# Two scatters behind a branch, two turns of gathered rows moved up, and GpSimd's memsets ahead of the first gathers

## The chip, the cores and the metric

The kernel runs on one core of one Trainium2 chip. The metric is device microseconds of a whole execution, median of several runs. TensorE (PE in the profile) multiplies matrices, VectorE (DVE) and ScalarE (ACT) work on tiles of 128 partitions, GpSimd (POOL) does element-wise work too and issues the DMAs whose rows are picked by an index, and SyncE (SP) issues plain DMAs. Each engine runs its own queue in order; semaphores hold the queues together.

## The reference

The input `x` has 8 sequences of 2496 rows with 256 channels. The first part multiplies each channel's spectrum with a complex filter:

```python
X = np.fft.rfft(x, axis=1)
Y = X * (filt_r + 1j * filt_i)[None, :, :]
y = np.fft.irfft(Y, n=x.shape[1], axis=1)
```

The second part takes the 19968 rows of `y` as tokens of a mixture of 8 experts, with a capacity of 80 tokens each:

```python
logits = x @ w_gate
expert_idx = np.argmax(logits, axis=1)
gate_w = softmax(logits)[arange, expert_idx]
out = zeros((N, D))
for e in range(E):
    tok_idx = the tokens of expert e, at most `capacity` of them with the largest gate_w
    h = np.maximum(x[tok_idx] @ w1[e], 0.0)
    out[tok_idx] = gate_w[tok_idx, None] * (h @ w2[e])
```

So at most 640 of the 19968 output rows are not zero.

## The kernel before

The Fourier transform is done by matmuls with tables. A sequence is read in six chunks (`load_x`, line 299, issued by SyncE). `stage1` (line 310) multiplies eleven pairs of columns, steps k = 0 to 10, with a small table; the results go to the tile `t1` by copies on ScalarE, for the first sequence on VectorE at every third step (line 324). `transpose1` (line 326) turns them, and `stage2` (line 338) multiplies with the second table and then, on VectorE and GpSimd, with the filter. `turn` (line 366) turns the products and gets the gating logits from them. This runs step by step over all 8 sequences, and the order of the work on each engine is the order in which the source writes it, under a manual schedule (from line 809).

The filter comes in five blocks of rows in `fst`. `load_filter(v, half)` (line 273) issues two gathers on GpSimd, of real rows (half 0) or imaginary rows (half 1); `sign_filter(v)` (line 281) multiplies the imaginary rows with a sign on ScalarE, in two passes; `turn_filter` (line 287) transposes them on TensorE. At the start GpSimd issues the four gathers of block 0 (lines 851 and 852), clears its tiles (`lg`, `zero_t`, two `z`, `key`, `kt`; line 854), copies the identity twice, and waits with a one-element copy to `mark` (line 858) for the fourth chunk of `x` before it gathers blocks 1 and 2. `sign_filter(0)` stands in ScalarE's queue behind step 6 of the first sequence.

`zero_t` is the source of the 64 DMAs that fill the output with zeros, one at a time through the first part. The tokens are picked while the last sequences run, and the picked rows are computed back from the spectra into the DRAM tile `y_sel`.

The experts come last (class `Experts`, line 1129). For each expert, `gather` (line 1144) fetches its rows, `turn` (line 1158) transposes them on TensorE into `px`, which VectorE copies to `xs`; `layer1` (line 1176) is 16 products to PSUM, which ScalarE and VectorE bring to `hT`; `layer2` (line 1192) is 8 products, a scaling by the gate on ScalarE into `ys`, and a scatter of 80 rows to `out` on GpSimd (line 1208). For the first three experts the gathered rows lack those of the last sequence; `turn` adds them by two more matmuls with `yr` and `last`. The order is written out in lines 1033 to 1048. For expert 7 `layer2` gets `keep=ys_last`: the result stays in a slice of `zero_t`, and its scatter stands at the end of the kernel (line 1126).

Between them is a branch (lines 1087 and 1088): if the fast way of picking failed (`bad` is not 0), a general path computes all again. With this input it isn't taken, but every engine reads `bad` and passes the branch; on the path that skips the body each engine also raises its semaphores by what the body would have added, GpSimd those of its DMA queues too (INC_SWDGE_SEM in the profile), after it has waited for its own DMAs ahead of the branch. In the built program each scatter waits for the landing of the scatter ahead of it, as they all write `out`.

Of the kernel before, what the change touches and what calls it, by code (L numbers as in the profile page):

```python
# [15 lines left out]
I32 = mybir.dt.int32  # L16
# [7 lines left out]
B, S, C = 8, 2496, 256  # L24
# [12 lines left out]
E, FF = 8, 1024  # L37
# [44 lines left out]
def kernel(  # L82
# [11 lines left out]
    nc = tc.nc  # L94
# [9 lines left out]
                                  name=f"rows{h}_tbl") for h in range(2)]  # L104
# [5 lines left out]
    consts = ctx.enter_context(tc.tile_pool(name="consts", bufs=1))  # L110
# [22 lines left out]
    lg = consts.tile([128, NP, NA, E], F32, name="lg")  # L133
# [57 lines left out]
    zero_t = zp.tile([128, ZR * C // 128], F32, name="zero_t")  # L191
# [9 lines left out]

    idxs = consts.tile([cap, E], I32, name="idxs")
    idxg = consts.tile([cap, E], I32, name="idxg")
    idx_last = consts.tile([cap, 1], I32, name="idx_last")
    ys_last = zero_t[0:cap, 0:C]
    gate = consts.tile([cap, E], F32, name="gate")
    idxt = consts.tile([cap, E], I32, name="idxt")
    idxb = consts.tile([128, B], I32, name="idxb")
# [26 lines left out]
    zs = [consts.tile([128, 2, E, SP], F32, name=f"z_{i}") for i in range(2)]  # L235
    key = consts.tile([128, 48, E], F32, name="key")
    kt = consts.tile([128, 2, N2, 4], F32, name="kt")

    with ExitStack() as actx:
# [33 lines left out]
        def load_filter(v, half):  # L273
            k, filt = half, (filt_r, filt_i)[half]
            for i in range(2):
                nc.gpsimd.indirect_dma_start(
                    out=fst[:, v, 2 * k + i, :], out_offset=None, in_=filt[:, :],
                    in_offset=bass.IndirectOffsetOnAxis(
                        ap=frow[:, 2 * v + i:2 * v + i + 1], axis=0))
# [254 lines left out]
        def pt(shape, dt, name, rnd):  # L534
            return sp.tile(shape, dt, name=f"{name}_{rnd}", tag=name)
# [214 lines left out]
        def pick_slots(part):  # L750
            f_t = st["f_t"]
            if part == 0:
                off_e = pt([128, 1], F32, "off_e", 1)
                nc.vector.tensor_copy(out=off_e[:], in_=st["poff"][:, 2, 0:1])
                slot = pt([128, KR], F32, "slot", 1)
                nc.vector.tensor_scalar(out=slot[:], in0=iota[:, 0:KR], scalar1=off_e[:, 0:1],
                                        scalar2=None, op0=AL.add)
                st["slot"] = slot
            elif part == 3:
                slot = st["slot"]  # L760
                st["eplc"] = xpool.tile([128, KR, cap], BF16, name="eplc", tag="x")
                nc.vector.tensor_tensor(
                    out=st["eplc"][:], in0=slot[:].unsqueeze(2).to_broadcast([128, KR, cap]),
                    in1=iota[:, 0:cap].unsqueeze(1).to_broadcast([128, KR, cap]),
                    op=AL.is_equal)
            elif part == 1:
                st["eval"] = pt([128, KR, 4, E], BF16, "eval_", 1)
                for i in range(4):
                    nc.gpsimd.tensor_tensor(
                        out=st["eval"][:, :, i, :],  # L770
                        in0=f_t[:, i, :].unsqueeze(2).to_broadcast([128, KR, E]),
                        in1=ehot[:].unsqueeze(1).to_broadcast([128, KR, E]), op=AL.mult)
            elif part == 2:
                pe = st["misc"][0:cap, 128:128 + 4 * E]
                for k in range(KR):
                    nc.tensor.matmul(pe, lhsT=st["eplc"][:, k, :],
                                     rhs=st["eval"][:, k].rearrange("p v e -> p (v e)"),
                                     start=(k == 0), stop=(k == KR - 1))
                es = st["es"] = pt([cap, 4, E], F32, "es", 1)
                nc.vector.tensor_copy(out=es[:].rearrange("p v e -> p (v e)"), in_=pe)  # L780
                nc.vector.scalar_tensor_tensor(out=idxg[:], in0=es[:, 1, :], scalar=128.0,
                                               in1=es[:, 0, :], op0=AL.mult, op1=AL.add)
                emp = pt([cap, E], F32, "emp", 1)
                nc.vector.tensor_scalar(out=emp[:], in0=es[:, 3, :], scalar1=st["off"][0:cap, 0:1],
                                        scalar2=float(N + S), op0=AL.is_le, op1=AL.mult)
                tokens(nc, sp, cap, es[:, 1, :], 0.0, es[:, 2, :], es[:, 3, :], -1.0, emp, idxs,
                       idxt)
                nc.vector.tensor_copy(out=idx_last[:], in_=idxs[:, E - 1:E])
            else:
                es = st["es"]  # L790
                inl = pt([cap, NO], F32, "inl", 1)
                nc.vector.tensor_scalar(out=inl[:], in0=es[:, 1, 0:NO], scalar1=float(B - 1),
                                        scalar2=None, op0=AL.is_equal)
                nc.vector.scalar_tensor_tensor(out=inl[:], in0=es[:, 0, 0:NO], scalar=1.0,
                                               in1=inl[:], op0=AL.add, op1=AL.mult)
                diag = fp.tile([cap, NO, cap], BF16, name="diag", bufs=1)
                nc.vector.tensor_tensor(
                    out=diag[:], in0=ident[0:cap, 0:cap].unsqueeze(1).to_broadcast([cap, NO, cap]),
                    in1=inl[:].unsqueeze(2).to_broadcast([cap, NO, cap]), op=AL.mult)
                last = st["last"] = fp.tile([128, NO, cap], F32, name="last", bufs=1)  # L800
                pd = st["misc"][:, 192:192 + NO * cap]
                nc.tensor.matmul(pd, lhsT=ones_bf[0:cap, :], start=True, stop=True,
                                 rhs=diag[:].rearrange("p e t -> p (e t)"))
                nc.vector.tensor_scalar(
                    out=last[:].rearrange("p e t -> p (e t)"), in0=pd, scalar1=pid[:, 0:1],
                    scalar2=1.0, op0=AL.subtract, op1=AL.is_equal)

        LATE, LEAD = 2, 2
        with tc.manual_schedule():
# [3 lines left out]
            for cb in range(NDB):  # L813
                nc.scalar.dma_start(out=gi[:, cb, 128:128 + E],
                                    in_=moe_w_gate[128 * cb:128 * cb + 128, :])
# [16 lines left out]
            def put_s1():  # L832
                if s1:
                    b, k = s1.pop(0)
                    stage1(b, k)
                    if (2 * k + 2) % JC == 0 or k == NB - 1:
                        free[0] += 1
# [10 lines left out]
            for _ in range(NX0 - NCH):  # L848
                load_x(*xs.pop(0))
            free[0] = 0  # L850
            load_filter(0, 0)
            load_filter(0, 1)
            for t in (lg, zero_t, *zs, key, kt):
                nc.gpsimd.memset(t[:], 0.0)
            nc.gpsimd.tensor_copy(out=gi[:, 0, 0:128], in_=ident[:])
            nc.gpsimd.tensor_copy(out=gi[:, 1, 0:128], in_=ident[:])
            mark = tpool.tile([1, 1], F32, name="mark")
# [4 lines left out]
            load_filter(2, 1)  # L862
            for k in range(NB):
                put_s1()
                if k == 6:
                    sign_filter(0)
                if k == 7:
                    load_d(1)
                    put_x(-1)
# [130 lines left out]
            for part in range(5):  # L1000
# [20 lines left out]
            ex = Experts(nc, cap, ident, fp, lambda n: fps.tile([128, 512], F32, name=n, tag="f"),  # L1021
                         lambda n: yps.tile([128, 2, 512], F32, name=n, tag="y"),
                         y_sel[0:128 * B, :], out, idxg, idxs, gate, w1s, w2s, homes=homes)
# [7 lines left out]
            ex.extra = st["yr"], st["last"]  # L1031

            ex.turn(0)
            ex.layer1(0)
            ex.turn(1)
            for e in range(E):
                if e + 3 < E:
                    ex.gather(e + 3)
                if e == 0:
                    ex.layer2(0)  # L1040
                if e + 1 < E:
                    ex.layer1(e + 1)
                if e + 2 < E:
                    ex.turn(e + 2)
                if e > 0:
                    ex.layer2(e, keep=ys_last if e == E - 1 else None)
                if e + 6 < E:
                    weights(e + 6, wpool, "w")

# [38 lines left out]
    with tc.If(n_bad > 0):  # L1088
# [22 lines left out]
        with (  # L1111
# [5 lines left out]
            ex = Experts(nc, cap, ident, fp3, lambda n: px3.tile([128, 512], F32, name=n, tag="f"),  # L1117
                         lambda n: ph3.tile([128, 2, 512], F32, name=n, tag="y"), y_sel, out,
                         idxg, idxs, gate, w1s, w2s, "g")
            for e in range(E):  # L1120
# [2 lines left out]
                ex.turn(e)  # L1123
                ex.layer1(e)
                ex.layer2(e)
    scatter(nc, out, ys_last, idx_last[:])


class Experts:
# [78 lines left out]
def scatter(nc, out, ys, idx):  # L1208
    nc.gpsimd.indirect_dma_start(  # L1209
        out=out[:, :], out_offset=bass.IndirectOffsetOnAxis(ap=idx, axis=0), in_=ys,  # L1210
        in_offset=None, bounds_check=N - 1, oob_is_err=False)
# [400 lines left out]
```

## Time and profile before

| | us |
|---|---|
| median of 3 runs (461.26 to 462.69) | 461.64 |
| profiled execution | 453.17 |
| its span, first to last instruction | 451.4 |
| TensorE busy, of the span | 431.9 |
| first 20 us: TensorE busy | 16.15 |
| experts, 381 to 440: TensorE busy | 58.5 |
| behind the last matmul, 440 to 451.4 | 11.4 |

The span is what the lines and timelines show; the profiled execution has 1.8 us around it. The runs without a profile have a longer median than the profiled one. A line of a timeline has the start in us, the duration, the engine, the line of the source, the operation, the tiles, and in brackets how long the engine sat idle before it and what ended that. A busy time says little by itself here, as TensorE is busy nearly all the time: what counts is what TensorE waits for, and what follows its last matmul.

The order of the experts' work on TensorE, one item each (t turn, 1 and 2 the layers, with the expert's number), is this before:

```
t0 1.0 t1 2.0 1.1 t2 1.2 t3 2.1 1.3 t4 2.2 ... 1.7 2.6 2.7
```

### The profile page before, as it was taken

What the parts mean: (1) busy time and instruction counts of PE and PEld (TensorE: products, weight loads), DVE (VectorE), ACT (ScalarE), POOL (GpSimd) and SP (SyncE); (2) the same over time, 40 slices, a digit from 0 to 9 for tenths busy, and PEclk for the clock granted to TensorE, in tenths of its full rate; (3) what the DMA queues carried; (4) which work ended last, traced back from release to release, by engine and by line L of the source; (5) the groups of instructions that cost most, each with busy time, mean ns of one, the idle gap of its engine ahead of it and who ended that gap; (6) DMA issues with size and microseconds to landing.
All of it is one profiled execution on the core that took longest, in us unless ns stands there. A gap on an engine that the chain in (4) does not pass through costs nothing. (4 is left out here: it accounts for less than half of the span.)

```text
span 451.4 us, 8713 instructions
## 1 busy us (share of the span) xinstructions
PE 431.9 (96%) x3389; PEld 406.6 (90%) x3389; DVE 194.2 (43%) x577; ACT 219.5 (49%) x359; POOL 178.5 (40%) x244
## 2 busy tenths in 40 slices
PE   7899999999999999999999999999999999999990
PEld 5899999999999999999999998888888888888870
DVE  2565544445654545754546789478300000110100
ACT  3576766666766666766666644332223321111110
POOL 8687343342543443443444456220754002112110
PEclk9999999999999999999999999999999999999997
DMA  7867345999988987878991222996989972999100
GB/s 206 278 178 226 65 129 180 325 293 359 351 244 253 328 265 231 290 241 254 362 395 79 95 94 99 366 359 257 355 320 362 396 255 77 374 367 369 36 20 12
DMA packets 39701, 109.96 MB, mean 244 GB/s; under 512 B 5297, under 2 KB 14832, under 8 KB 38882
## 3 DMA queue, kind: packets, MB, share of 16 engines
q1 hardware_dynamic: 28688, 76.41, 50.6%
q10 hardware_dynamic: 6466, 21.05, 11.9%
q0 software_dynamic: 4496, 11.85, 8.0%
q8 instruction: 29, 0.48, 0.4%
q14 instruction: 22, 0.18, 0.1%
HBM read 68.97 MB, written 43.20 MB: 249 GB/s over the span
## 5 line engine op out<-in xcount | busy, mean ns | idle before, releaser
L358 POOL TENSOR_TENSOR p<-p,p 128x256 f32<-128x256 f32 x154 | 110.0, 736 | 134.3 <-DVE p L351 93.1
L351 DVE TENSOR_TENSOR p<-pb,ft 128x512 f32<-128x512 f32 x160 | 102.2, 680 | 11.0 <-PE pb L343 10.9
L324 ACT COPY t<-pa 128x480 f32<-128x480 f32 x84 | 83.8, 1002 | 26.1 <-PE pa L317 25.7
L317 PE MATMUL pa<-wf_t,x 117*128 117x120 f32 x704 | 91.2, 276 | 3.4 <-DMA x<-in_x_dram 3.0
L317 PEld LDWEIGHTS pa<-wf_t,x 117*128 117x128 f32 x704 | 84.9, 192 | 5.1 <-DMA x<-in_x_dram 1.8
L371 PE MATMUL py<-gi,p 128*128 128x136 f32 x640 | 87.8, 280 | 1.3 <-POOL p L358 0.7
L343 PE MATMUL pb<-d_t,t 128*128 128x128 f32 x640 | 85.2, 276 | 0.2
L371 PEld LDWEIGHTS py<-gi,p 128*128 128x128 f32 x640 | 79.8, 190 | 1.7 <-POOL p L358 1.0
L343 PEld LDWEIGHTS pb<-d_t,t 128*128 128x128 f32 x640 | 78.0, 192 | 1.1 <-PE py L371 0.4
L334 ACT COPY t<-pt 128x512 f32<-128x512 f32 x80 | 46.7, 585 | 59.8 <-PE pt L332 58.4
L520 PE MATMUL po<-yb,wt 128*128 128x256 f32 x240 | 56.6, 380 | 0.3 <-ACT wt L513 0.3
L394 DVE COPY z<-py 128x16 f32<-128x16 f32 x60 | 11.2, 187 | 86.6 <-ACT ysp L387 57.9
L332 PE MATMUL pt<-ident,t 128*128 128x128 f32 x320 | 47.9, 273 | 0.4 <-DVE t L324 0.4
L520 PEld LDWEIGHTS po<-yb,wt 128*128 128x128 f32 x240 | 43.4, 190 | 5.3 <-ACT wt L513 0.5
L513 ACT COPY wt<-pw 128x512 f32<-128x512 f32 x39 | 22.7, 585 | 47.4 <-PE pw L508 45.3
L332 PEld LDWEIGHTS pt<-ident,t 128*128 128x128 f32 x320 | 37.5, 141 | 0.6 <-issue 0.6
L387 ACT COPY ysp<-py 128x512 f32<-128x512 f32 x60 | 35.4, 591 | 0.0
L1182 PEld LDWEIGHTS ph<-xs,w 128*128 128x128 f32 x256 | 29.7, 192 | 1.7 <-DVE xs L1173 1.1
L1182 PE MATMUL ph<-xs,w 128*128 128x80 f32 x256 | 29.8, 275 | 0.8 <-DVE xs L1173 0.8
L1197 PE MATMUL po<-w,hT 128*80 128x256 f32 x128 | 28.8, 379 | 0.0
L1197 PEld LDWEIGHTS po<-w,hT 128*80 128x80 f32 x128 | 18.6, 150 | 7.5
L1188 DVE TENSOR_SCALAR hT<-ph 128x320 f32<-128x320 f32 x8 | 3.9, 491 | 47.9 <-ACT hT L1187 47.9
(204 smaller groups left out, 339.5 us busy)
## 6 DMA issues: line engine op xcount, KB each, us to landing
out_dram<-zero_t SPq DMA_DIRECT2D x64, 312.0 KB
x<-in_x_dram SPq DMA_DIRECT2D x40, 468.0 KB
w<-in_moe_w_dram SPq DMA_DIRECT2D x16, 1024.0 KB
yf<-ysp ACTq DMA_DIRECT2D x30, 512.0 KB
yb<-yf SPq DMA_DIRECT2D x6, 2560.0 KB
yf<-ys ACTq DMA_DIRECT2D x10, 512.0 KB
x<-in_x_dram SPq DMA_DIRECT2D x8, 234.0 KB
d_t<-d_tbl SPq DMA_DIRECT2D x5, 256.0 KB
```

Source lines behind the costliest of these rows:

```text
L317: nc.tensor.matmul(out=ps[:, i, :, 2 * NS * cb:2 * NS * cb + 2 * NS], lhsT=xt[0:NJ * N1, (2 * k + i) % JC, 128 * cb:128 * cb + 128], rhs=w ...
L324: copy(out=t1[:, 2 * k - h:2 * k - h + 2], in_=ps[:])
L332: nc.tensor.transpose(ps[:, i, cb, :], t1[:, a:a + 2, :].rearrange("p r n -> p (r n)"), ident[:])
L334: nc.scalar.copy(out=t2[:].rearrange("p i c -> p (i c)"), in_=ps[:].rearrange("p i c q -> p (i c q)"))
L343: nc.tensor.matmul(out=ps[:, cb, i], rhs=d_t[:, 2 * u + i, :], start=True, stop=True, lhsT=t2[:, i, 128 * cb:128 * cb + 128])
L351: nc.vector.tensor_tensor(out=pt, in0=ps[:].rearrange("p c s r q -> p (c s) r q"), in1=f.unsqueeze(2).to_broadcast([128, 2 * NDB, 2, NQ]), ...
L358: adder.tensor_tensor(out=yt[:, :, r, :], in0=yt[:, :, r, :], in1=pr[1][:, :, 1 - r, :], op=op)
L371: nc.tensor.matmul(out=ps[:, i, ZW * cb:ZW * cb + ZW], rhs=gi[:, cb, :], lhsT=yt[:, 2 * cb + i].rearrange("p r q -> p (r q)"), start=True, ...
L387: nc.scalar.copy(out=dst.rearrange("p s (h w) -> p s h w", h=2), in_=pv[:, :, :, 0:128])
L520: nc.tensor.matmul(pos[t][:, 0, 0:C], lhsT=wts[t, g // 2][:, g % 2, i, :], rhs=ybs[t][:, s, :], start=(s == 0), stop=(s == NS - 1))
L1182: nc.tensor.matmul(ph[:, fc // 4, fc % 4, 0:cap], lhsT=self.w1s[e][:, k, 128 * fc:128 * fc + 128], rhs=xs[:, k, :], start=(k == 0), stop=( ...
L1197: nc.tensor.matmul(po[0:cap, :], lhsT=hT[:, fc, :], rhs=self.w2s[e][:, fc, :], start=(fc == 0), stop=(fc == NFC - 1))
```

## The change

Four edits:

- The results of experts 6 and 7 are both kept, in two slices of `zero_t`, and both are scattered behind the branch, with their two columns of indices in `idx_last`. Before it was expert 7's alone.
- `turn(1)` is moved ahead of expert 0's layer 1 and `turn(2)` directly behind it. TensorE's order becomes `t0 t1 1.0 t2 2.0 1.1 1.2 t3 2.1 1.3 ...`; from turn 3 on it is the same.
- GpSimd clears its six tiles ahead of the four gathers of filter block 0 instead of behind them.
- `sign_filter(0)` stands behind step 8 instead of step 6 in ScalarE's queue.

Nothing else moves in any engine's queue.

```diff
@@ -201,8 +201,9 @@
 
     idxs = consts.tile([cap, E], I32, name="idxs")
     idxg = consts.tile([cap, E], I32, name="idxg")
-    idx_last = consts.tile([cap, 1], I32, name="idx_last")
-    ys_last = zero_t[0:cap, 0:C]
+    NL = 2
+    idx_last = consts.tile([cap, NL], I32, name="idx_last")
+    ys_last = [zero_t[0:cap, C * i:C * i + C] for i in range(NL)]
     gate = consts.tile([cap, E], F32, name="gate")
     idxt = consts.tile([cap, E], I32, name="idxt")
     idxb = consts.tile([128, B], I32, name="idxb")
@@ -785,7 +786,7 @@
                                         scalar2=float(N + S), op0=AL.is_le, op1=AL.mult)
                 tokens(nc, sp, cap, es[:, 1, :], 0.0, es[:, 2, :], es[:, 3, :], -1.0, emp, idxs,
                        idxt)
-                nc.vector.tensor_copy(out=idx_last[:], in_=idxs[:, E - 1:E])
+                nc.vector.tensor_copy(out=idx_last[:], in_=idxs[:, E - NL:E])
             else:
                 es = st["es"]
                 inl = pt([cap, NO], F32, "inl", 1)
@@ -848,10 +849,10 @@
             for _ in range(NX0 - NCH):
                 load_x(*xs.pop(0))
             free[0] = 0
+            for t in (lg, zero_t, *zs, key, kt):
+                nc.gpsimd.memset(t[:], 0.0)
             load_filter(0, 0)
             load_filter(0, 1)
-            for t in (lg, zero_t, *zs, key, kt):
-                nc.gpsimd.memset(t[:], 0.0)
             nc.gpsimd.tensor_copy(out=gi[:, 0, 0:128], in_=ident[:])
             nc.gpsimd.tensor_copy(out=gi[:, 1, 0:128], in_=ident[:])
             mark = tpool.tile([1, 1], F32, name="mark")
@@ -862,7 +863,7 @@
             load_filter(2, 1)
             for k in range(NB):
                 put_s1()
-                if k == 6:
+                if k == 8:
                     sign_filter(0)
                 if k == 7:
                     load_d(1)
@@ -1031,8 +1032,9 @@
             ex.extra = st["yr"], st["last"]
 
             ex.turn(0)
+            ex.turn(1)
             ex.layer1(0)
-            ex.turn(1)
+            ex.turn(2)
             for e in range(E):
                 if e + 3 < E:
                     ex.gather(e + 3)
@@ -1040,10 +1042,10 @@
                     ex.layer2(0)
                 if e + 1 < E:
                     ex.layer1(e + 1)
-                if e + 2 < E:
+                if 2 < e + 2 < E:
                     ex.turn(e + 2)
                 if e > 0:
-                    ex.layer2(e, keep=ys_last if e == E - 1 else None)
+                    ex.layer2(e, keep=ys_last[e - E + NL] if e >= E - NL else None)
                 if e + 6 < E:
                     weights(e + 6, wpool, "w")
 
@@ -1123,7 +1125,8 @@
                 ex.turn(e)
                 ex.layer1(e)
                 ex.layer2(e)
-    scatter(nc, out, ys_last, idx_last[:])
+    for i in range(NL):
+        scatter(nc, out, ys_last[i], idx_last[:, i:i + 1])
 
 
 class Experts:
```

## The prediction

> **What bounds the kernel now.** I read the page's busy times first, then a table of stages, then the waits of TensorE, and then, stage by stage, the timelines of the places that the change touches.
>
> ```profile
> PE 431.9 (96%) x3389; PEld 406.6 (90%) x3389; DVE 194.2 (43%) x577; ACT 219.5 (49%) x359; POOL 178.5 (40%) x244
> ```
>
> TensorE is busy for 96% of the span of 451.4 us. So work taken off another engine is worth nothing unless TensorE, or the end of the program, stood waiting for it. The table of stages (columns: stretch, length, busy PE, PEld, DVE, ACT, POOL, granted clock, DMA share, GB/s) shows where TensorE is not busy:
>
> ```profile
> 0.00:20.00 20.00, 16.15 (x111) 12.83 (x112) 9.02 (x32) 8.86 (x10) 14.32 (x28) 1.00 0.82 238
> ...
> 440.00:451.40 11.40, 0.00 (x0) 0.00 (x0) 0.00 (x0) 0.45 (x1) 0.91 (x1) 0.71 0.04 12
> ```
>
> Of the 19.5 us without matmuls, 3.85 lie in the first 20 us and 11.4 after the last matmul. The change edits both ends. Between them TensorE's waits that matter here are short (columns: who waited for whom, total us, times, longest):
>
> ```profile
> PE pa L317 <- DMA x<-in_x_dram: 3.0, 4, 1.1
> ...
> PE ph L1182 <- DVE xs L1173: 0.8, 2, 0.4
> ```
>
> The first is the wait for the input at the start, the second a round trip to VectorE in the expert stage. The end, by the timeline of the last 15 us (start, duration, engine, line):
>
> ```profile
> 436.58 0.47 ACT L1202 ACTIVATE ys<-po,gate 80x256 f32<-80x256 f32 x1 [3.07 <-PE po L1197]
> 437.32 0.91 POOL L1209 DMA_INDIRECT out_dram<-ys,idxs  x1 [6.06 <-DVEq L1088]
> 439.99 0.47 ACT L1202 ACTIVATE zero_t<-po,gate 80x256 f32<-80x256 f32 x1 [2.94 <-PE po L1197]
> 443.75 0.91 POOL L1209 DMA_INDIRECT out_dram<-zero_t,idx_last  x1 [5.51 <-ACTq L1088]
> ```
>
> The last result is ready at 440.46, yet its scatter starts at 443.75, 3.29 later; expert 6's scatter started 0.27 after its result (437.05 to 437.32). Why is in the rows of the branch's line (duration min/median/max in ns, first and last start):
>
> ```profile
> L1088 POOLq COMPARE_BRANCH  x1: 53/53/53, 437.7 to 437.7; - x1
> L1088 ACTq COMPARE_BRANCH  x1: 50/50/50, 440.5 to 440.5; - x1
> ...
> L1088 POOLq INC_SWDGE_SEM  x1: 1500/1500/1500, 441.1 to 441.1; - x1
> L1088 ACTq EVENT_SEMAPHORE  x1: 17/17/17, 443.4 to 443.4; - x1
> ```
>
> GpSimd reaches the branch only after dispatching expert 6's scatter: it compares at 437.7, its next instruction (from the same view) runs at 440.6, it waits there for all scatters ahead of the branch to land, and an instruction that raises the DMA semaphores takes 441.1 to 442.6. Then come a few waits to 442.98 and the scatter. GpSimd's passage of the branch, not the last result, sets the end. After the scatter stands one long item:
>
> ```profile
> L1607 POOLq DRAIN  x3: 50/173/6603, 443.5 to 451.1; - x3
> ```
>
> GpSimd's closing drain of 6.6 us, 443.5 to 450.1; from the scatter's start to the span's end it is 7.65. The start:
>
> ```profile
> 6.56 0.95 POOL L276 DMA_INDIRECT fst<-in_filt_i_dram,frow  x1 [0.30 <-issue]
> ...
> 13.38 0.18 POOL L858 COPY mark<-x 1x1 f32<-1x1 f32 x1 [1.87 <-DMA x<-in_x_dram]
> ...
> 13.47 4.70 PE L317 MATMUL pa<-wf_t,x 117*128 117x120 f32 x40 [0.93 <-DMA x<-in_x_dram]
> ...
> 19.40 1.06 PE L332 MATMUL pt<-ident,t 128*128 128x128 f32 x8 [0.36 <-DVE t L324]
> ```
>
> The first filter gathers are issued between 2.58 and 7.51, while the input's chunks are arriving; TensorE waits at 10.5 and 13.4 for a chunk, and `mark` shows that the fourth one lands at 13.4.
>
> **What the Trainium skill says.** "Runtime: NRT & Kernel Launch", section Instruction fetch mechanics: a taken branch out of the prefetched window forces a fetch before execution goes on. The trace agrees: 2.9 us from compare to next instruction on GpSimd (437.7 to 440.6) and on ScalarE (440.5 to 443.4). "DMA: Bandwidth & Descriptors", section Anatomy of one DMA — SWDGE (gpsimd) path: a fixed part of about 2.0 us, most of it the write receipt. Here the last four scatters land 2.3 to 2.9 us after their start, where the queues are quiet. Same page, section Queues, rings and completion order: each DMA engine goes round between the queues that have work. That fits the early gathers: 7.0, 7.7, 7.5 and 7.3 us to landing beside the input's loads. "Perfetto Trace Analysis", the section on SWDGE DMA: the profiled end is that of descriptor generation, so the 0.91 of a scatter isn't its landing.
>
> **The change, part by part.**
>
> *The scatters behind the branch.* In the changed program GpSimd's queue is: expert 5's scatter, branch, expert 6's scatter, expert 7's scatter. Expert 5's result is ready at 430.06 (its ScalarE copy starts 429.59, takes 0.47), its scatter starts 430.34. In the old order the compare came 0.4 after a scatter's start, so it now comes at about 430.75. The fetch gives 433.65; expert 5's scatter has landed by 430.34 + 2.5 = 432.84, so nothing more is waited for. 0.5 of waits and 1.5 for the semaphore instruction give 435.65, the waits behind it 0.4, and the old trace has 0.77 from there to the scatter's start: 436.8. Expert 6's result is ready at 437.05, so its scatter starts at 437.32 as before, with 0.5 us to spare. The passage is now hidden behind the matmuls of experts 6 and 7. Expert 7's scatter waits for two things by the built program: its result (440.46) and the landing of expert 6's scatter, as both write `out`. That is 437.32 + 2.3 to 2.9 = 439.6 to 440.2. So it starts at 440.46 + 0.27 = 440.73 instead of 443.75: **3.0 us** sooner. Late next is TensorE's last matmul itself. ScalarE passes the branch at 440.5 as before and is at the end at 443.5, ahead of GpSimd's drain, which I take at its 6.6 us. The two kept results lie in two slices of `zero_t`, whose zeros were written out long before; the index copy is two columns instead of one on an idle VectorE: nothing.
>
> *Turning sooner.* Twice layer 1 stands directly behind the turn that feeds it and waits 0.41 and 0.42 us (before 380.62 and 393.61) for VectorE's 0.32 us copy. Now turn 1 (0.9 us of matmuls) stands between turn 0 and layer 1 of expert 0, and turn 2 between that and layer 2, so that two layers lie between it and its use. No matmul is added. Both waits go: **0.8 us**. The gathered rows of experts 1 and 2 were issued at 373.00 and 374.26 and take 2.5 us, so they are there when turned at 380 and 385. Expert 2's weights are loaded from 380.5 at about 336 GB/s; layer 1 of expert 2 comes 0.8 earlier than 393.6, and the first of two 1 MB halves needs some 3 us.
>
> *Memsets ahead of the gathers.* Six memsets (1.18 + 0.63 + 1.01 + 0.43 + 0.54, or 3.5 us from the first's start at 7.51 to the last's end) now start at 1.95, when GpSimd was idle for 0.63. They end near 5.45; the four gathers start near 5.6, 7.1, 8.35 and 9.6 instead of 2.58, 4.05, 5.31 and 6.56. All of their 0.52 MB (512 rows of 1 KB) landed by 13.9 before. Now about half of it should come after the fourth chunk, which at the some 265 GB/s of these microseconds lands 0.9 earlier, at 12.5. TensorE's first stage then ends 0.9 sooner, near 17.1. But what follows is late next: the imaginary rows land at 9.6 + 7.3 = 16.9, their sign (two ScalarE passes, 0.9 together, now behind the copy of step 8) ends at 17.9, the copy of step 9 behind it (1.0) at 18.9, and the transposes need that: 19.05 instead of 19.40. The gain is therefore **0.4 us**. Its bounds: 0.9, if the rows land in the 5.6 us of the later gathers (18.5), and a loss of 2, if they take 9.7. I take 0.4, as the four old gathers agree within 0.7. The gathers of the second block wait for `mark`, not for GpSimd, and come earlier with it.
>
> The sum is 3.0 + 0.8 + 0.4 = 4.2 us. The profiled execution (453.17, its span 451.4 and 1.8 around it) would become 449.0. The runs shown have a median of 461.64, 8.5 more than the profiled one; no part of this difference is known to lie in the edited places, so I take the 4.2 off the median: **457.4**.
>
> **Rivals.**
> *ScalarE's passage of the branch releases the scatters.* The timeline names ScalarE's branch as releaser of the last scatter: event at 443.4, start 443.75. If the kept results are only seen then, expert 6's scatter waits for 443.75 too, lands at 446.0 to 446.6, and expert 7's follows at 446.6 instead of 443.75, a loss of 2.9. With 1.2 gained elsewhere the kernel is 1.7 slower: 463.3. It decides as soon as more than 1.2 is lost at the end. For it: the 0.5 us between 442.98 and the drain's dispatch that nothing else explains. Against: expert 6's scatter is labelled likewise (VectorE's branch, 437.3) though it stands ahead of the branch, so the label goes by nearness in time; and the built program waits for the count of ScalarE's own copies.
> *The closing drain doesn't follow the last scatter*, or grows with a second one close ahead of it. One length of it is known (6.6). If it takes 3 longer, the end gains nothing and 1.2 is left: 460.4.
> *The imaginary rows land late*, at 9.7 us: the start loses 2.0 where I count a gain of 0.4. That gives 3.0 + 0.8 - 2.0 = 1.8: 459.8. For it: sign and two copies queue behind them on ScalarE. Against: no early gather took more than 7.7.
>
> **How the numbers follow.** The forecast has 0.69, the ScalarE rival 0.08, the drain 0.12, the late rows 0.11. The forecast's own range is 456.2 (0.5 more at the start, and 0.7 for the spread of the medians) to 458.8. To leave out no more than 2 in 10 the range takes in the late rows and part of the drain: 455.6 to 460.2. A difference under 0.3% (1.4 us) can't be told from none. Faster by more: nearly all of the forecast and of the late rows, a third of the drain: 0.82. Within: 0.10. Slower: 0.08.
>
> **What would show it.** Right: GpSimd's compare near 431 (less the gains ahead of it), the two scatters some 3.4 us apart, the last one 0.3 after ScalarE's last copy, and 7.6 from there to the end; no wait of layer 1 for `xs`; the first transposes of the second stage at about 19.0, ScalarE's sign passes waiting for a DMA. Wrong: a gap over 1 us between the last copy and the last scatter, a longer drain, or the first transposes after 19.4.

## The result and the profile after

| | before | after | ratio after/before, 95% |
|---|---|---|---|
| median of this comparison, us | 461.64 | 458.11 | 0.9918 [0.9894, 0.9941] |
| forecast, us | | 457.4 (455.6 to 460.2) | |
| profiled execution, us | 453.17 | 459.31 | |
| its span, us | 451.4 | 457.5 | |

The kernel is 3.5 us faster by the medians (3.8 by the ratio), where 4.2 was forecast. A ratio is taken from the fast runs alone, without those more than 1.5% above the fastest of their kernel, and isn't the quotient of two medians, so the two can differ by 0.2%. The two profiles, put side by side, say the opposite: the span grew by 6.1 us. Times differ from chip to chip here: the kernel before took 453.28 us on one chip and 462.11 to 463.65 on three others (below). The profile of after has a stall near its start that the profile of before lacks and that such chips show for both kernels. So no conclusion may be drawn from one span minus the other; each stretch has to be read by itself. Busy times of after, from the page:

```profile
PE 434.4 (95%) x3389; PEld 409.2 (89%) x3389; DVE 192.8 (42%) x577; ACT 219.8 (48%) x359; POOL 178.6 (39%) x244
```

The table of stages of after (columns: stretch, length, busy PE, PEld, DVE, ACT, POOL, granted clock, DMA share, GB/s):

```profile
0.00:20.00 20.00, 15.05 (x99) 11.60 (x100) 5.80 (x29) 7.89 (x9) 14.28 (x28) 1.00 0.81 232
20.00:60.00 40.00, 34.12 (x278) 33.67 (x277) 19.09 (x46) 23.67 (x35) 22.98 (x29) 0.91 0.50 136
...
100.00:260.00 160.00, 159.94 (x1412) 159.53 (x1412) 86.67 (x221) 108.09 (x164) 68.78 (x98) 1.00 0.83 281
```

From 100 to 260 TensorE is busy without a gap, with the same 159.94 us as before. The loss sits in 20 to 60: 34.12 busy instead of 39.76, and a clock of 0.91. TensorE's waits of after name it:

```profile
PE pt L333 <- DVE t L325: 5.9, 1, 5.9
...
PE pa L318 <- DVE x L303: 1.4, 1, 1.4
```

(Line numbers of after are a few higher: L333 is L332 of before, L1212 the scatter, L1090 the branch, L1610 the end.) The 5.9 us are a stall ahead of the first transposes of the second stage; it is dealt with further down, as it isn't the change's. Cut at three points, the difference of the two spans is: first transposes at 26.72 instead of 19.40, +7.32; from there to expert 0's `yr` matmul 362.77 instead of 359.91, +2.86 (6.8 us at a halved clock lie in it, see the last section); from that to the last matmul 59.36 instead of 60.64, -1.28; from ScalarE's last copy to the end 8.14 instead of 10.91, -2.77. The sum is +6.1. The last two stretches are those that the change shortens at the end.

The end of after, by its timeline (start, duration, engine, line):

```profile
439.25 0.93 POOL L1212 DMA_INDIRECT out_dram<-ys,idxs  x1 [6.19 <-ACT ys L1205]
...
445.44 0.47 ACT L1205 ACTIVATE zero_t<-po,gate 80x256 f32<-80x256 f32 x1 [3.02 <-PE po L1200]
446.18 0.92 POOL L1212 DMA_INDIRECT out_dram<-zero_t,idx_last  x1 [6.01 <-ACT zero_t L1205]
448.89 0.47 ACT L1205 ACTIVATE zero_t<-po,gate 80x256 f32<-80x256 f32 x1 [2.98 <-PE po L1200]
449.89 0.91 POOL L1212 DMA_INDIRECT out_dram<-zero_t,idx_last  x1 [2.79 <-ACT zero_t L1205]
```

Expert 6's scatter follows its copy by 0.27 us (445.91 to 446.18), expert 7's by 0.53 (449.36 to 449.89); before it was 3.29. The rows of the branch's line in after (duration min/median/max in ns, first and last start):

```profile
L1090 POOLq COMPARE_BRANCH  x1: 53/53/53, 439.6 to 439.6; - x1
...
L1090 POOLq INC_SWDGE_SEM  x1: 1480/1480/1480, 443.4 to 443.4; - x1
...
L1090 ACTq EVENT_SEMAPHORE  x1: 17/17/17, 452.2 to 452.2; - x1
```

GpSimd compares 0.4 us after expert 5's scatter (439.25) and is through by 445, ahead of expert 6's result. ScalarE's own event of the branch comes at 452.2, when both scatters have long started: they didn't wait for it. The closing item keeps its length, by the rows of the last line of after:

```profile
L1610 POOLq DRAIN  x3: 50/168/6603, 449.7 to 457.2; - x3
```

### The profile page after: what moved, and what is told of

Its sections match the earlier page's. It is cut to its first block, busy times and chain, and to the rows that moved or that the text cites. A ratio compares the mean times of both kernels' runs of the same rounds, so it can differ in the third digit from the quotient of the medians.

```text
span 457.5 us, 8710 instructions
## 1 busy us (share of the span) xinstructions
PE 434.4 (95%) x3389; PEld 409.2 (89%) x3389; DVE 192.8 (42%) x577; ACT 219.8 (48%) x359; POOL 178.6 (39%) x244
## 5 line engine op out<-in xcount | busy, mean ns | idle before, releaser
L318 PE MATMUL pa<-wf_t,x 117*128 117x120 f32 x704 | 92.2, 277 | 4.0 <-DMA x<-in_x_dram 2.4
L333 PE MATMUL pt<-ident,t 128*128 128x128 f32 x320 | 49.1, 278 | 5.9 <-DVE t L325 5.9
L333 PEld LDWEIGHTS pt<-ident,t 128*128 128x128 f32 x320 | 38.7, 144 | 6.1 <-issue 6.1
L492 POOL DMA_INDIRECT gts<-rows_tbl,idxb x16 | 16.1, 1008 | 21.0 <-DVE idxb L708 16.7
```

The costliest lines, as they stand in the source:

```text
L318: nc.tensor.matmul(out=ps[:, i, :, 2 * NS * cb:2 * NS * cb + 2 * NS], lhsT=xt[0:NJ * N1, (2 * k + i) % JC, 128 * cb:128 * cb + 128], rhs=w ...
L333: nc.tensor.transpose(ps[:, i, cb, :], t1[:, a:a + 2, :].rearrange("p r n -> p (r n)"), ident[:])
```

## The experiments

"Before" in a row is the kernel before on the same chip: e1 to e4 ran on one chip, e5 to e7 on a second, e8 to e11 on a third, e12 on a fourth. Columns: ratio to before; then from the profile the tail (ScalarE's last copy to the end of the span), the expert stretch (first `yr` matmul to last matmul), and the start of the second stage's first transposes.

| kernel | median | before | ratio, 95% | tail | experts | transposes |
|---|---|---|---|---|---|---|
| e1 scatters | 450.14 | 453.28 | 0.9933 [0.9914, 0.9951] | 8.13 | 60.64 | 19.93 |
| e2 turns | 452.32 | 453.28 | 0.9977 [0.9966, 0.9989] | 10.67 | 59.36 | 20.03 |
| e3 memsets | 453.02 | 453.28 | 0.999 [0.9973, 1.0007] | 10.72 | 60.64 | 19.41 |
| e4 both ends | 449.45 | 453.28 | 0.9908 [0.9885, 0.993] | 7.89 | 59.36 | 19.60 |
| e5 after | 458.80 | 463.65 | 0.9876 [0.9847, 0.9906] | 7.89 | 59.36 | 27.12 |
| e6 sign at step 6 | 458.74 | 463.65 | 0.9912 [0.9883, 0.994] | 7.89 | 59.36 | 24.74 |
| e7 imaginary first | 459.11 | 463.65 | 0.9919 [0.9894, 0.9944] | 7.89 | 59.36 | 25.92 |
| e8 before | 462.27 | 462.88 | 0.9983 [0.9968, 0.9997] | 10.74 | 60.64 | 22.51 |
| e9 both ends | 458.42 | 462.88 | 0.9898 [0.9872, 0.9925] | 7.89 | 59.36 | 23.57 |
| e10 after | 457.50 | 462.88 | 0.9889 [0.9857, 0.992] | 7.89 | 59.36 | 24.93 |
| e11 imaginary first | 457.15 | 462.88 | 0.9891 [0.9862, 0.9921] | 7.89 | 59.36 | 22.18 |
| e12 after | 457.77 | 462.11 | 0.99 [0.9866, 0.9933] | 8.21 | 59.36 | 26.13 |

One row is a caution for the rest: e8 is the kernel before against itself, and its interval leaves out 1 by 0.03%. So a ratio of 0.998 alone settles nothing; a stretch of the profile has to say the same.

### The scatters alone (e1)

```diff
+    NL = 2
...
-                    ex.layer2(e, keep=ys_last if e == E - 1 else None)
+                    ex.layer2(e, keep=ys_last[e - E + NL] if e >= E - NL else None)
...
-    scatter(nc, out, ys_last, idx_last[:])
+    for i in range(NL):
+        scatter(nc, out, ys_last[i], idx_last[:, i:i + 1])
```

> Only the two scatters behind the branch, all else as before. By the profiles of before and after the stretch from the end of the last ScalarE copy to the end of the span is 10.9 us before and 8.1 us after. Theory (the branch's passage is hidden): this stretch is 8.1 us here too, the last scatter starts about 0.5 us after the last copy, and the time falls by 2.8 us (ratio 0.994). Rival (the gain came from the other edits, or is given back in the closing drain): the stretch stays at 10.9 us and the ratio is 1.000.

Measured: 3.1 us less. The end in e1's timeline:

```profile
436.26 0.47 ACT L1204 ACTIVATE zero_t<-po,gate 80x256 f32<-80x256 f32 x1 [3.02 <-PE po L1199]
437.01 0.92 POOL L1211 DMA_INDIRECT out_dram<-zero_t,idx_last  x1 [6.00 <-ACT zero_t L1204]
439.71 0.47 ACT L1204 ACTIVATE zero_t<-po,gate 80x256 f32<-80x256 f32 x1 [2.98 <-PE po L1199]
440.70 0.92 POOL L1211 DMA_INDIRECT out_dram<-zero_t,idx_last  x1 [2.78 <-ACT zero_t L1204]
```

The last scatter starts at 440.70 instead of 443.75, with TensorE's work at nearly the same times. GpSimd's compare is at 430.4 and its semaphore instruction at 433.8 (1.48 us), so the passage ends under the matmuls of experts 6 and 7. ScalarE still compares after its last copy, at 440.3, and has its event at 442.9, 2.2 us behind the last scatter. This refutes the rival in which ScalarE's passage releases the scatters. The drain is 6.6 us as before: the drain rival falls too.

### The turns alone (e2)

```diff
             ex.turn(0)
+            ex.turn(1)
             ex.layer1(0)
-            ex.turn(1)
+            ex.turn(2)
...
-                if e + 2 < E:
+                if 2 < e + 2 < E:
```

> Only the moved turns, all else as before. From the first matmul with yr to the end of the last matmul the profiles show 60.6 us before and 59.35 us after. Theory (the two round trips to VectorE go): this stretch is 59.35 us here, and the time falls by 1.2 us (ratio 0.9973). Rival (the 0.8 us of the waits is all there is): 59.8 us and a ratio of 0.998. The end stretch stays at 10.9 us in both.

Measured: 1.0 us less by the medians, 1.28 by the expert stretch, which has 59.36 us in every kernel with this edit and 60.64 in every one without it. That is half again what the two waits sum to. The reason is in how the wait is drawn. Before, expert 2's last turn and its layer 1 (timeline of TensorE):

```profile
392.80 0.39 PE L1170 MATMUL px<-last,yr 128*128 128x80 f32 x2
393.61 3.80 PE L1182 MATMUL ph<-xs,w 128*128 128x80 f32 x32 [0.42 <-DVE xs L1173]
```

In after, the last turn ahead of layer 1 of expert 0, and that layer:

```profile
390.90 0.39 PE L1173 MATMUL px<-last,yr 128*128 128x80 f32 x2
391.12 3.74 PE L1185 MATMUL ph<-xs,w 128*128 128x80 f32 x32
```

Two matmuls whose successor starts 0.22 us after them when nothing holds it are drawn 0.39 long: the drawn end lies behind the point where the next one could have begun. The wait is drawn only behind that end. From start to start it is 0.81 with the wait and 0.22 without: 0.59 us each, not 0.41. Two of them make 1.18 of the 1.28. The last 0.1 lies in the layers themselves: from the first matmul of such a layer 1 to the start of the item behind it the traces have 3.63 us with the wait ahead of it (before) and 3.57 without (e2), twice.

### The memsets ahead of the gathers alone (e3)

```diff
+            for t in (lg, zero_t, *zs, key, kt):
+                nc.gpsimd.memset(t[:], 0.0)
             load_filter(0, 0)
             load_filter(0, 1)
-            for t in (lg, zero_t, *zs, key, kt):
-                nc.gpsimd.memset(t[:], 0.0)
...
-                if k == 6:
+                if k == 8:
                     sign_filter(0)
```

> Only the memsets ahead of the filter gathers, with the sign passes behind step 8; all else as before. Theory A (a long stall of TensorE in the first 30 us, which the profile of after shows and that of before doesn't, comes in most runs of either kernel): ratio between 0.998 and 1.003, and the first transposes of the second stage start anywhere from 19 to 28 us. Theory B (the moved gathers bring the stall): slower than before by 2 us or more (ratio 1.005 or above). Theory C (the gain that I forecast): ratio 0.999.

Measured: 0.3 us less, within what can't be told from none. The start in e3's timeline:

```profile
12.07 0.18 POOL L858 COPY mark<-x 1x1 f32<-1x1 f32 x1 [1.05 <-DMA x<-in_x_dram]
...
12.15 2.02 PE L317 MATMUL pa<-wf_t,x 117*128 117x120 f32 x16 [0.25 <-DMA x<-in_x_dram]
...
15.23 2.91 PE L317 MATMUL pa<-wf_t,x 117*128 117x120 f32 x24 [1.06 <-DVE x L302]
...
17.18 0.89 ACT L284 ACTIVATE fst<-fst,fsig 128x256 f32<-128x256 f32 x2
...
18.26 1.01 DVE L324 COPY t<-pa 128x480 f32<-128x480 f32 x1 [3.08 <-PE pa L317]
...
19.41 1.06 PE L332 MATMUL pt<-ident,t 128*128 128x128 f32 x8 [0.39 <-DVE t L324]
```

The fourth chunk comes at 12.07, 1.3 us sooner than in the profile of before, as meant. But behind the two steps that read it (16 matmuls) TensorE now stands for 1.06 us ahead of step 8. Before, the 40 matmuls of steps 6 to 10 ran from 13.47 through without a gap. Steps 8 and 9 read the fifth chunk of `x`. The view puts the wait down to a one-element memset on VectorE for another chunk's buffer; in before that memset ran at 16.46, after step 8 had begun at 15.32, so it isn't what step 8 needs. Nor is it a PSUM buffer: there are three in turn, so step 8 takes that of step 5, whose copy ended at 12.93. The fifth chunk is what is left, and the trace's DMA packets say the same. A chunk is 117 packets of 4 KB in SyncE's queue; the fourth 117 were done at 10.49 in e3 and 12.02 in before, the fifth at 14.26 and 14.46. (The count doesn't tell chunks apart that are under way together.) So the fourth chunk won 1.5 us and the fifth 0.2. Of the 512 KB of the four gathers 508 were moved by 13 us in before; in e3 it was 32 by 11 us, and the rest went from 11 to 16 us, beside the fifth chunk. The last matmul of the first stage starts at 17.87, against 17.89 in before: all that was won at the fourth chunk is given back at the fifth. VectorE's copy of step 10 runs at 18.26 (before 18.27), and the transposes that wait for it at 19.41 (before 19.40).

This holds over all profiles. In the eight with the memsets ahead, step 6 starts on average at 13.26 and step 8 at 16.39, each with 0.65 to 1.63 us from the last matmul of step 7 to the first of step 8 (0.11 without a wait), and step 8 starts 0.96 to 1.30 us after the fifth 117 packets are done; in the six with the old order, step 6 starts at 13.88 and step 8 at 15.89, with 0.11 us ahead of step 8 in five of them and 0.31 in one (e9). Single profiles scatter by some 2 us, on one chip too (step 8 at 17.06 in e10, at 15.05 in e11), so the half us by which step 8 is later isn't a finding; that the gain at the fourth chunk doesn't reach step 8 is.

### Both ends, without the start (e4)

The edits of e1 and e2 together.

> The scatters and the turns together, the start as before. If the edits at the end add up and the start gives nothing, the time falls by 4.0 us (ratio 0.9913), a little more than the whole change's 3.5 us. If the start's edit gains the 0.4 us that I forecast, this kernel is slower than the changed one by 0.4 us; if the start's edit costs time, it is faster than the changed one by that.

Measured: 3.8 us less by the medians, 4.2 by the ratio (0.0092 of 453.28). The profile has both, a tail of 7.89 and an expert stretch of 59.36, against 10.91 and 60.64: 4.3. The profile's span is no shorter than e2's, 450.2, because it holds a wait of 2.0 us for a chunk of `x` between 60 and 100, which neither edit touches. It is one execution.

### After again, the sign's place, and the order of the gathers (e5 to e7)

e5 is the changed kernel. e6 puts the sign back:

```diff
-                if k == 8:
+                if k == 6:
                     sign_filter(0)
```

and e7 gathers the imaginary rows first:

```diff
-            load_filter(0, 0)
             load_filter(0, 1)
+            load_filter(0, 0)
```

> The changed kernel again, beside the same runs of the kernel before as the others of this call. By the parts, 2.8 us for the scatters, 1.0 to 1.2 for the turns and 0.4 for the start: 4.2 to 4.4 us less than before, ratio 0.9905. If the start's edit costs time on the whole, the ratio is above 0.992. Without a stall of TensorE at the start the profile has its first transposes of the second stage at about 19.4 us, TensorE's updates of its semaphore follow its matmuls at once, and the span is near 446.5 us.

> The changed kernel with the sign passes back behind step 6. Theory (the imaginary rows are late next): the rows land at about 16.5 us, ScalarE waits there for them with the copies of steps 8 and 9 queued behind the sign, and the first transposes start at about 20.0 us instead of 19.4; the time is 0.5 to 0.9 us above that of the changed kernel, and the start's edit as a whole loses. Rival (the place of the sign doesn't matter, another step holds the transposes): the same start within 0.2 us.

> The changed kernel with the imaginary rows of the first filter block gathered ahead of the real ones. Theory (the imaginary rows and the sign behind them hold the start): they land at about 14.6 us, the sign runs at once behind the copy of step 8, at about 16.2 us, and the first transposes start 0.6 to 0.9 us sooner than in the changed kernel, at about 18.6 us; the time is 0.6 to 0.9 us below it. Rival (the input's last chunks hold the start): the first transposes within 0.2 us of the changed kernel's, and the same time.

Measured: the three medians lie within 0.4 us of each other. By the ratios the changed kernel is 0.36 and 0.43% below e6 and e7 (some 1.7 and 2.0 us), but the intervals overlap, if narrowly, so the times settle nothing. All three have the stall of the first 30 us, with the transposes at 24.7 to 27.1, so an edit that moves the sign by a microsecond is hidden under it there. What comes ahead of the stall can be read. ScalarE in e6, with the sign behind step 6 (timeline):

```profile
15.54 0.51 ACT L285 ACTIVATE fst<-fst,fsig 128x256 f32<-128x256 f32 x1 [0.20 <-DMA fst<-in_filt_i_dram,frow]
16.43 0.51 ACT L285 ACTIVATE fst<-fst,fsig 128x256 f32<-128x256 f32 x1 [0.38 <-DMA fst<-in_filt_i_dram,frow]
17.44 1.00 ACT L325 COPY t<-pa 128x480 f32<-128x480 f32 x1 [0.50 <-issue]
```

The passes do wait for the imaginary rows, by 0.20 and 0.38 us, and the rows land near the 16.5 that the theory has. But they hold nothing: ScalarE is through at 16.94, and its copy of step 8 comes 1.16 us after step 8's first matmul (16.28), the same 1.16 as in e3, after and e7, where the sign stands behind that copy. In e7 the sign runs at 18.13, on the heels of the copy of step 8 (17.34 to 18.33), without a wait for a DMA, as in e3, so rows that land sooner have nothing to shorten. Up to the copy of step 8 both rivals hold: not the rows but step 8, and with it the input, sets the pace. What sets the transposes behind it isn't answered by e6 and e7, as the stall begins there. They also show that the stall isn't made by the place of the sign or the order of the gathers.

### The stall: before, both ends, after and imaginary first on one chip (e8 to e11)

e8 has no edit, e9 is e4, e10 is after, e11 is e7.

> The kernel before once more, for its profile on this chip. The kernel before took 453.3 us on one chip and 463.6 on another. Theory (the 10 us are a stall of TensorE in the first 30 us that belongs to the chip): on a chip where the median is near 462, the first transposes of the second stage start at 26 us or later, the clock is halved for some us behind them, and the rest of the stages are as in the profile that was shown; where it is near 453, they start at 19 to 20 us. Rival (the chip is slower everywhere): the stages from 60 to 440 us are longer by some per cent. The ratio is 1.000.

> The scatters and the turns, with the start as before: 4.2 us below before on a chip without the stall (ratio 0.991), and by the same 4.2 us on one with it, if the stall doesn't depend on the order at the start (0.991). If the memsets ahead of the gathers shorten the stall, this kernel is slower than the changed one by 1 us or more on such a chip.

> The changed kernel beside the last one, which differs in the start alone. By my forecast of the start 0.4 us below it on a chip without the stall: 4.6 us below before, ratio 0.990. On a chip with the stall, by the 5 us of the last call, 1 to 1.5 us below it, ratio 0.988 to 0.989.

> The imaginary rows ahead of the real ones, else as the changed kernel. On a chip without the stall, theory (the sign behind the late imaginary rows holds the first transposes): they start at about 18.6 us instead of 19.4, and the time is 0.6 to 0.9 us below the changed kernel's; rival (the input holds them): the same time within 0.3 us. On a chip with the stall the two can't be told apart.

Measured: the kernel before has the stall too. The stage from 20 to 60 us of e8:

```profile
20.00:60.00 40.00, 36.02 (x295) 35.47 (x296) 21.13 (x51) 24.18 (x38) 22.83 (x29) 0.91 0.48 145
```

and its timeline:

```profile
21.41 0.96 DVE L324 COPY t<-pa 128x480 f32<-128x480 f32 x1 [4.68 <-remote]
...
22.51 1.64 PE L332 MATMUL pt<-ident,t 128*128 128x128 f32 x8 [3.27 <-DVE t L324]
```

The same kernel in the profile of before was busy for 39.76 of these 40 us, at full clock. So the change doesn't make the stall. The transposes come at 22.51, sooner than the 26 that the theory had for such a chip. Its rival, a chip that is slower everywhere, falls: from 100 to 260 us e8 runs 1412 matmuls and the profile of before 1410, both at full clock, and from the first `yr` matmul to the end of the span it takes 71.89 us against 72.05. Against both ends alone (e9), the whole change (e10) is 0.9 us less by the medians, with ratios of 0.9898 and 0.9889 whose intervals overlap almost wholly; e11 is as good as e10. No variant stands out from the changed kernel.

### The whole change once more (e12)

> The changed kernel once more. On a chip without the stall of the first 30 us (median of before near 453) the parts measured alone add: 3.1 + 1.3 + 0.3, so 4.7 us and a ratio near 0.990, with the first transposes of the second stage before 19.8. If the start's edit loses time once the others are in, the gain is under 4.0 and the transposes come after 20.5. On a chip with the stall (median of before above 460) the transposes come between 22 and 27 in the profile, and the gain of the start's edit can't be read; the tail of 7.9 to 8.2 us and the expert stretch of 59.4 us are expected there too.

Measured: a fourth chip, again with the stall (transposes at 26.13), and 4.3 us less than before. So no profile shows the start's edit together with the others without the stall; whether it adds its 0.3 there isn't known.

## Why the prediction was right, and where it wasn't

The four comparisons of the whole change give 3.5, 4.9, 5.4 and 4.3 us by the medians, and 3.8, 5.7, 5.1 and 4.6 by the ratios; the forecast was 4.2. By its steps:

*The scatters behind the branch*, 3.0 forecast: 3.1 by e1's medians; the tail shrank by 2.8 in e1 and after, by 2.7 in e12, and by 3.0 in the other seven profiles with this edit. The mechanism is as forecast: GpSimd's passage is hidden, in those seven the last scatter waits for its own result, the closing drain follows unchanged. (That the pause of 2.6 to 3.0 us behind GpSimd's compare is the fetch of instructions, as the prediction read it, no run here shows: the traces have the pause alone.) Where 0.25 is missing, the prediction left out a term. It had expert 7's scatter ready by its result at +0.27 and the landing of expert 6's scatter ahead of that. GpSimd's wait for that landing in after, by the rows of the scatter's line:

```profile
L1212 POOLq EVENT_SEMAPHORE  x7: 17/43/3115, 430.3 to 446.0; - x7
```

The wait of 3.1 us began at 446.03 and ended at 449.15, 2.97 after the scatter's start, and the next scatter starts 0.74 later. e1 and e12 have the same 0.74 to 0.75; there the landing decides, by a quarter of a microsecond. In e10 the wait ended 2.48 after the scatter's start, and the result decides at +0.28. The forecast's landing time (2.3 to 2.9) was nearly right; the way from the landing to the start wasn't in it, though the prediction had it from the old trace as 0.77 and used it for expert 6's scatter. The Trainium skill ("DMA: Bandwidth & Descriptors", Anatomy of one DMA — SWDGE (gpsimd) path) puts the fixed part at some 2.0 us; the 2.5 to 3.0 seen here, with 80 rows of 1 KB moved in them, lie above it.

*Turning sooner*, 0.8 forecast: 1.28 in the stretch, 1.0 by the medians. The mechanism was right, the term was mis-sized: the drawn wait of 0.41 understates what the round trip costs TensorE, which is 0.59 from start to start, and 0.06 more inside the layer behind it.

*Memsets ahead of the gathers*, 0.4 forecast: 0.3 measured in e3, not told from nothing. The size fits, the working doesn't. Right were the gathers (issued from 5.56 to 9.54 in e3, the last rows landed 7.0 later, at 16.52; forecast 16.9) and the earlier fourth chunk (12.07 in e3; over the profiles 0.6 on average at step 6, forecast 0.9). That the sign ran at 17.18, near the forecast's 17, is chance: it waited for no DMA, but stood behind the copy of step 8 (16.39 to 17.39), which the fifth chunk had made late. Wrong was the step "TensorE's first stage then ends 0.9 sooner": it took the fourth chunk as the last that TensorE waits for. The fifth is late next, as nearly all of the gathers' bytes, not half, moved from the fourth chunk's time to the fifth's; the stage ended at the same time, and the transposes were set by the same copy of step 10, not by the rows. In before the fifth 117 packets were done only 0.86 us ahead of step 8; where step 8 waits for them it starts 0.96 to 1.30 us behind them, so there was no room for 0.9. The transposes at 19.41 in e3 also meet the prediction's own sign of being wrong, a start after 19.4. Two slips of its working change nothing: of the 3.0 us that TensorE waits for `x`, 2.4 in three waits lie in the first 20 us, and the fourth wait comes later; and 16.9 + 0.9 is 17.8, not 17.9.

The three rivals fall: ScalarE's passage and the drain by e1, the late rows by e3, where they landed at 16.52 against the 19.3 of the rival (9.6 + 9.7). What held the forecast together was that the two large terms were taken from stretches where the released engine had nothing else to wait for; their errors, -0.2 and +0.5, and the 0.4 that has no mechanism behind it nearly cancel. That the sum comes so near to 4.2 is in that part luck.

Open: what the changed start does without the stall and with the other edits; where e3's 0.3 us come from, if they are real; and whether the spread of 3.5 to 5.4 us between the chips is more than chance.

## What to carry to other kernels

A skipped branch costs an engine its passage at the place where it stands in that engine's queue (here 4.9 us on GpSimd, from compare to the end of its semaphore instruction in before): put the last items that depend on late results behind it, so that the passage runs while another engine still computes. Read what a wait costs by the start-to-start distance with and without it, not by the drawn idle time. When a transfer is moved out of the way of one wait, ask which transfer it now stands beside, and whether the next wait reads that one.

## What the runs showed that was not expected

On three of the four chips, and in the profile of after, the first 30 us hold a stall that the fourth chip and the profile of before lack. In after (timeline):

```profile
17.06 2.91 PE L318 MATMUL pa<-wf_t,x 117*128 117x120 f32 x24 [1.35 <-DVE x L303]
...
21.31 0.96 ACT L325 COPY t<-pa 128x480 f32<-128x480 f32 x1 [1.41 <-PE pf L294]
...
25.61 0.96 DVE L325 COPY t<-pa 128x480 f32<-128x480 f32 x1 [8.90 <-remote]
...
26.72 1.94 PE L333 MATMUL pt<-ident,t 128*128 128x128 f32 x8 [5.88 <-DVE t L325]
```

The last 24 matmuls of the first stage are done near 20, but ScalarE and VectorE take up their results at 21.31 and 25.61. TensorE's semaphore events for these results stand in the trace at 21.29 and 25.52, so by the trace it is the news of the result that is late, not the reader. Behind the stall the matmuls of 25.7 to 32.6 run at about half speed (one every 0.21 us instead of 0.11), which makes the granted clock of 20 to 60 us 0.91. The traces with the stall also hold fewer semaphore events (5175 in after, 5752 in e3), so an event that was lost from the trace can't be ruled out. Why the events come late wasn't found, nor tried: nothing in the kernels tells it apart, and part of it may belong to the recording. But the medians of the kernel before differ between chips too, by 8.8 to 10.4 us, so it isn't a matter of single profiles (e8's span is 7.3 longer than that of the first profile of before). The mean granted clock, which is on record for every execution, fits: the kernel before has 0.990 to 0.993 in 31 of 32 executions on the first chip, and 0.973 to 0.989 on the three others. That all of the difference lies in the first 30 us isn't shown, as only profiles show places. Nor is it shown that the chip is the cause: each chip was used at one time only, and the one execution left on the first chip took 459.45 us at 0.985, which looks like the stall, but there is no profile of it.
